# Cutting the last product of a kernel, and one early multiply, in two halves

## The chip, the cores and the metric

The kernel runs on one core of one Trainium2 chip. The metric is the device time of one execution in microseconds (us). The time of the kernel before is a median of 304.57 us over three runs (304.38 to 305.19).

## The reference

Eight batches of eight heads attend in chunks of 64 tokens. The result, 4608 rows of 512, goes through a bilinear feed-forward layer.

```python
scores = scale * np.matmul(q_c, k_c.transpose(0, 1, 2, 4, 3))     # chunks of 64
attn = softmax(scores)                                            # cut: max, exp, sum
out = np.matmul(attn, v_c)
x = out.transpose(0, 2, 1, 3).reshape(B * S, H * D)               # 4608 x 512
result = ((x @ w_a) * (x @ w_b)) @ w_out                          # d_ff = 1536
```

## The kernel before

The tokens are worked on in units of 256 and blocks of 512. TensorE (PE) does all products. From block 1 on, the output product of a block is a form of 2x2 block multiplication with seven products (`part(n, th)`, n from 0 to 6), whose sums are kept in the banks A, B and C of PSUM, the memory that TensorE writes its sums to. For the last block it is done for each half of 128 rows (`th`) by itself, which the code calls `one`.

The first place that the change touches is the end of the attention of a unit. Both VectorE multiplies write into `xT`, the feed-forward product's input; `m` runs over its four slices of 128 features, and the feed-forward product accumulates over these four slices (`kt`).

```python
def values(U):
    ...                                        # av[cl]: attention times v, in PSUM
    for cl in range(2):
        x = x_tiles[K][:, :, 256 * u:256 * u + 256]
        nc.vector.tensor_tensor(
            out=x.rearrange("p m (g c s) -> p m g c s", g=2, c=2)[:, :, :, cl, :],
            in0=av[cl],
            in1=rs[:, cl].rearrange("p m (g s) -> p m g s", g=2),
            op=MULT,
        )
```

The second place is the end of the kernel. The loop that comes last is `for n in (1, 2, 4, 3, 5, 6): for th in range(2): ends[th].part(n, th)`, so the last piece of work is n = 6 with th = 1:

```python
def part(self, n, th):
    ...                                        # t, a, w: bank, left and right operand
    c0 = 0 if one else th * 256
    for kt in range(HFT):                      # HFT = 6
        nc.tensor.matmul(
            t[:, c0:c0 + 256],
            a[:, kt, th * 128:th * 128 + 128],
            w[:, kt],
            start=n in (0, 4) and first and kt == 0,
            stop=last and kt == HFT - 1,
            skip_group_check=True,
        )
    if not last:
        return
    ...                                        # n = 0 to 4
    elif n == 5:
        ...                                    # the right columns of o0, on ScalarE
        for c in [th] if one else range(2):
            store(self.K, 0, c, self.o0[:, c])
    else:
        nc.vector.tensor_scalar(
            out=rows(self.o1, lo), in0=halves(self.C), scalar1=OUT_SCALE,
            scalar2=None, op0=MULT,
        )
        for c in [th] if one else range(2):
            store(
                self.K, 1, c, self.o1[:, c], lo if one else slice(0, DM),
                nc.scalar if one and th else nc.sync,
            )
    ...                                        # n = 3: right columns of o1, stored; C += u
```

The softmax here doesn't subtract the row's maximum and nothing guards it: scores larger than these inputs give would overflow.

## Time and profile before

| what | value | where it is read |
|---|---|---|
| span of the profiled execution | 301.92 us | head of the page |
| PE busy | 291.9 us, 97% | part 1 of the page |
| share of PE in the chain that ended last | 83% | part 4 |
| first feed-forward matmul | 17.68 us | timeline |
| PE idle for GpSimd's wb cast | 0.28 us at 32.84 | timeline |
| last product, first matmul to the end of the span | 3.91 us | timeline, span |

Three parts of the page of the kernel before: its head, its busy times, and its chain by engine.

```profile
span 301.9 us, 8590 instructions
...
PE 291.9 (97%) x3521; PEld 231.6 (77%) x3521; DVE 212.5 (70%) x341; ACT 196.6 (65%) x355; POOL 193.5 (64%) x180
...
PE 83%; DMA 6%; DVE 3%; SPq 3%; ACT 1%; POOL 1%; issue 1%; DVEq 0%; ACTq 0%
```

Next is the timeline of the kernel before, cut to the lines that matter for the front. The columns are the start, the duration (both us), the engine, the source line, the operation, output and inputs, the shapes, and the count of merged instructions. In square brackets are the idle time of the engine before it, and what ended that.

```profile
16.24 0.69 DVE L337 TENSOR_TENSOR xT<-pb,ln 128x512 f16<-128x512 f32 x1 [0.31 <-ACT ln L305]
...
16.94 0.69 DVE L337 TENSOR_TENSOR xT<-po,ln 128x512 f16<-128x512 f32 x1
...
17.68 1.02 PE L389 MATMUL pb<-xT,wb 128*128 128x512 f16 x4 [0.38 <-DVE xT L337]
...
28.67 1.04 POOL L213 CAST q_raw<-st 128x1024 bf16<-128x1024 f32 x1 [1.10 <-DMA st<-in_q_dram]
...
32.84 1.04 PE L389 MATMUL pb<-xT,wb 128*128 128x512 f16 x4 [0.28 <-POOL wb L120]
32.85 1.04 POOL L120 CAST wa<-st 128x1024 f16<-128x1024 f32 x1
...
33.63 0.53 DVE L135 TENSOR_TENSOR t<-wa 128x512 f16<-128x512 f16 x1
...
33.95 1.04 PE L389 MATMUL pc<-xT,wa 128*128 128x512 f16 x4
```

The last multiply (L337) starts at 16.94 and ends at 17.63; PE starts 0.05 us later. At 32.84 PE sits idle for 0.28 us until GpSimd has cast a weight tile, and at 33.95 it starts 0.06 us after the end of the wa cast of 32.85. Such places are read by which wait ends last, not by how busy an engine is.

The next view is the table of stretches: the stretch, its length, the busy time of each engine with its count of instructions, the granted PE clock, the mean busy share of the 16 DMA engines (over 1 where packets overlap), and GB/s.

```profile
14.00:24.00 10.00, 9.47 (x76) 4.24 (x74) 5.26 (x9) 4.68 (x9) 6.41 (x7) 1.00 1.07 369
24.00:30.00 6.00, 6.00 (x32) 2.72 (x31) 4.11 (x7) 2.27 (x4) 3.14 (x3) 1.00 1.20 251
30.00:36.00 6.00, 5.66 (x68) 2.76 (x65) 5.04 (x8) 3.08 (x6) 4.30 (x4) 1.00 1.12 337
298.50:300.70 2.20, 0.33 (x4) 0.05 (x1) 0.56 (x2) 0.00 (x0) 0.00 (x0) 1.00 0.96 358
```

From 14 to 36 us the mean share of the DMA engines stays over 1, and from 298.5 to 300.7 it is 0.96, so they hardly rest. The last view is the timeline of the tail. An eviction there is VectorE's scaled copy of finished sums from PSUM to SBUF, from which the store is read.

```profile
298.01 0.82 PE L575 MATMUL pa<-wot,ab_sb 128*128 128x256 f16 x6
298.21 0.43 DVE L608 TENSOR_SCALAR o_sb<-po 128x256 f32<-128x256 f32 x1 [0.67 <-PE po L575]
298.87 0.42 DVE L608 TENSOR_SCALAR o_sb<-pa 128x256 f32<-128x256 f32 x1 [0.23 <-PE pa L575]
299.32 0.37 ACTq L523 DMA_DIRECT2D out_dram<-o_sb  x1
```

Six matmuls of 256 columns, the eviction of 128x256, and the issue of the last store at 299.32; the span ends at 301.92. In between lie the time to the store's first packet, its packets and the end of the program.

### The profile page before, as it was taken

The page shows a single profiled execution, that of the slowest core. Times are in us where ns is not written, and L with a number is a line of the kernel's source. Part 1 is how long each engine was busy: PE and PEld are TensorE (multiplying, and loading weights), DVE is VectorE, ACT ScalarE, POOL GpSimd, SP SyncE. Part 2 cuts the span into 40 slices and gives each one's busy share as a digit, 9 for nine tenths or more (in the row PEclk, how much of TensorE's full clock was granted, in tenths as well). Part 3 has the DMA queues.
Part 4 walks back from the last instruction along what each step waited for, and adds up shares of the span by engine and source line. Part 5 has one row for each costly group of instructions (what it writes and reads, how often), then busy time and mean ns, then how long its engine had stood idle before and what let it go on. Part 6 is the DMA issues. An engine that isn't in the chain of part 4 may idle for free.

```text
span 301.9 us, 8590 instructions
## 1 busy us (share of the span) xinstructions
PE 291.9 (97%) x3521; PEld 231.6 (77%) x3521; DVE 212.5 (70%) x341; ACT 196.6 (65%) x355; POOL 193.5 (64%) x180
## 2 busy tenths in 40 slices
PE   6799999999999999999999999999999999999995
PEld 2344467766588888888888888888888888888884
DVE  3456766866887696769676967796679667965773
ACT  2743567348387759676877687768776877567532
POOL 0665758996999688908890888088817801790560
PEclk9999999999999999999999999999999999999999
DMA  7999999999999999895959395949631001100025
GB/s 233 303 376 275 289 336 342 246 205 214 224 235 269 209 237 275 189 228 174 215 114 240 138 210 124 229 144 207 123 87 72 2 2 69 72 1 3 2 78 200
DMA packets 140983, 54.29 MB, mean 180 GB/s; under 512 B 117136, under 2 KB 135056, under 8 KB 140944
## 3 DMA queue, kind: packets, MB, share of 16 engines
q1 hardware_dynamic: 140800, 53.62, 70.3%
q8 instruction: 27, 0.44, 0.6%
q10 hardware_dynamic: 144, 0.13, 0.1%
q14 instruction: 12, 0.10, 0.1%
HBM read 37.75 MB, written 9.44 MB: 156 GB/s over the span
## 4 chain that ended last, share of the span: by engine, by line
PE 83%; DMA 6%; DVE 3%; SPq 3%; ACT 1%; POOL 1%; issue 1%; DVEq 0%; ACTq 0%
PE pb L439 19%; PE pc L439 12%; PE pa L439 12%; PE po L575 12%; PE pq L575 10%; PE pb L643 3%; DMA st<-in_moe_w_b_dram 3%; DMA st<-in_moe_w_a_dram 2%; PE po L389 2%; PE pc L389 2%; PE pa L389 2%; PE pq L389 2%; DMA st<-in_v_dram 2%; PE pt L328 2%; PE pt L295 2%; SPq L194 1%
## 5 line engine op out<-in xcount | busy, mean ns | idle before, releaser
L519 POOL TENSOR_TENSOR so<-ab_sb 128x512 f16<-128x512 f16 x23 | 27.4, 1191 | 68.6 <-DVE ab_sb L489 68.6
L439 PEld LDWEIGHTS <-t 128*128 128x128 f16 x504 | 48.3, 98 | 8.8 <-issue 2.3
L439 PE MATMUL pb<-s,wa 128*128 128x256 f16 x336 | 50.5, 273 | 0.0
L439 PE MATMUL pa<-xT,wb 128*128 128x256 f16 x336 | 50.4, 273 | 0.0
L477 DVE TENSOR_TENSOR c_sb<-pc,v_sb 128x512 f32<-128x512 f32 x42 | 28.9, 687 | 25.4 <-ACT v_sb L450 25.4
L575 PEld LDWEIGHTS <-ab_sb 128*128 128x128 f16 x384 | 37.6, 98 | 4.7 <-issue 0.4
L439 PEld LDWEIGHTS <-wb 128*128 128x128 f16 x336 | 32.9, 98 | 4.0
L439 PEld LDWEIGHTS <-wa 128*128 128x128 f16 x336 | 31.8, 98 | 4.2 <-issue 0.2
L489 DVE SCALAR_TENSOR_TENSOR ab_sb<-pc,c_sb 128x512 f16<-128x512 f32 x42 | 28.9, 689 | 7.8 <-PE pc L439 6.3
L450 ACT COPY u_sb<-pb 128x512 f32<-128x512 f32 x42 | 24.7, 588 | 14.8 <-PE pb L439 14.7
L489 DVE SCALAR_TENSOR_TENSOR ab_sb<-pb,b_sb 128x512 f16<-128x512 f32 x42 | 29.0, 689 | 6.1 <-PE pb L439 5.2
L457 ACT COPY pb<-pa 128x512 f32<-128x512 f32 x42 | 24.0, 573 | 10.7 <-PE pa L439 10.3
L575 PEld LDWEIGHTS <-so 128*128 128x128 f16 x288 | 28.1, 98 | 3.4
L450 ACT COPY b_sb<-pa 128x512 f32<-128x512 f32 x42 | 25.0, 595 | 7.1 <-PE pa L439 7.1
L478 DVE TENSOR_TENSOR pc<-pc,u_sb 128x512 f32<-128x512 f32 x42 | 28.9, 688 | 0.0
L519 POOL TENSOR_TENSOR so<-so,ab_sb 128x512 f16<-128x512 f16 x23 | 27.1, 1180 | 1.7
L450 ACT COPY v_sb<-pb 128x512 f32<-128x512 f32 x42 | 24.6, 587 | 5.0 <-PE pb L439 4.4
L519 POOL TENSOR_TENSOR ab_sb<-ab_sb 128x512 f16<-128x512 f16 x23 | 26.9, 1172 | 0.0
L519 POOL TENSOR_TENSOR so<-ab_sb,so 128x512 f16<-128x512 f16 x23 | 26.2, 1170 | 0.0
L337 DVE TENSOR_TENSOR xT<-pt,ln 128x512 f16<-128x512 f32 x29 | 18.8, 686 | 10.1 <-PE pt L328 6.7
L439 PE MATMUL pc<-s,t 128*128 128x256 f16 x168 | 25.2, 273 | 0.2 <-DVE ab_sb L489 0.2
L439 PE MATMUL pc<-xT,t 128*128 128x256 f16 x168 | 25.2, 272 | 0.1
(129 smaller groups left out, 576.9 us busy)
## 6 DMA issues: line engine op xcount, KB each, us to landing
out_dram<-o_sb SPq DMA_DIRECT2D x34, 256.0 KB, 2.3
st<-in_v_dram SPq DMA_DIRECT2D x32, 256.0 KB, 4.6
st<-in_k_dram SPq DMA_DIRECT2D x25, 256.0 KB, 4.6
st<-in_q_dram SPq DMA_DIRECT2D x23, 256.0 KB, 3.9
st<-in_moe_w_b_dram SPq DMA_DIRECT2D x6, 512.0 KB, 7.1
st<-in_moe_w_a_dram SPq DMA_DIRECT2D x6, 512.0 KB, 6.9
st<-in_moe_w_out_dram SPq DMA_DIRECT2D x6, 512.0 KB, 6.4
st<-in_q_dram SPq DMA_DIRECT2D x4, 512.0 KB, 5.4
```

Source lines behind the costliest of these rows:

```text
L295: nc.tensor.matmul(sm[cl][j * 64:j * 64 + 64, :], ones[cl * 64:cl * 64 + 64, :], E[cl * 64:cl * 64 + 64, j].rearrange("p m g s -> p (m g s)"),
L337: nc.vector.tensor_tensor(out=x.rearrange("p m (g c s) -> p m g c s", g=2, c=2)[:, :, :, cl, :], in0=av[cl], in1=rs[:, cl].rearrange("p m ...
L389: nc.tensor.matmul(ps[n], w_ab[n, i][:, kt, o:o + 128], xT[:, kt, c0:c1], start=(kt == 0), stop=(kt == NKT - 1),)
L439: nc.tensor.matmul(t[:, h * 256:h * 256 + 256], w[:, kt, h * 128:h * 128 + 128], x[:, kt], start=start and h == 0 and kt == 0, stop=h == 1 ...
L450: nc.scalar.copy(out=t, in_=src)
L457: nc.scalar.copy(out=self.B, in_=self.A)
L477: nc.vector.tensor_tensor(out=self.c, in0=self.C, in1=self.v, op=ADD)
L478: nc.vector.tensor_tensor(out=self.C, in0=self.C, in1=self.u, op=ADD)
L489: nc.vector.scalar_tensor_tensor(out=self.dst[:, :, c0:c0 + 256], in0=t.rearrange("p (h n) -> p h n", h=2), scalar=AB_SCALE, in1=o.rearran ...
L519: (eng or nc.gpsimd).tensor_tensor(out=o, in0=x0, in1=x1, op=op)
L575: nc.tensor.matmul(t[:, c0:c0 + 256], a[:, kt, th * 128:th * 128 + 128], w[:, kt], start=n in (0, 4) and first and kt == 0, stop=last and ...
L643: nc.tensor.matmul(out_ps[K, tg], ab_tiles[K][:, ft, tg * 128:tg * 128 + 128], wo_sb[:, ft], start=(ft == 0), stop=(ft == NFT - 1),)
```

## The change

Its intent is to shorten two waits. The first feed-forward matmuls should start when half of `xT`'s slices are there. At the end, the eviction and the store of the first 128 columns should overlap the product of the second 128 columns, so that only half an eviction and half a store remain after the last matmul.

```diff
         for cl in range(2):
             x = x_tiles[K][:, :, 256 * u:256 * u + 256]
-            nc.vector.tensor_tensor(
-                ...
-            )
+            for m in (slice(0, 2), slice(2, 4)) if (U, cl) == (1, 1) else [slice(0, 4)]:
+                nc.vector.tensor_tensor(
+                    out=x.rearrange("p m (g c s) -> p m g c s", g=2, c=2)[:, m, :, cl, :],
+                    in0=av[cl][:, m],
+                    in1=rs[:, cl, m].rearrange("p m (g s) -> p m g s", g=2),
+                    op=MULT,
+                )
 ...
-            for kt in range(HFT):
-                nc.tensor.matmul(
-                    t[:, c0:c0 + 256],
-                    ...
-                )
-            if not last:
+            end = n == 6 and one and th == 1
+            for cols in (slice(0, 128), slice(128, 256)) if end else [slice(0, 256)]:
+                for kt in range(HFT):
+                    nc.tensor.matmul(
+                        t[:, c0:c0 + 256][:, cols],
+                        a[:, kt, th * 128:th * 128 + 128],
+                        w[:, kt, cols],
+                        ...                              # start, stop as before
+                    )
+                if end:
+                    nc.vector.tensor_scalar(
+                        out=rows(self.o1, cols), in0=self.C[:, cols], scalar1=OUT_SCALE,
+                        scalar2=None, op0=MULT,
+                    )
+                    store(
+                        self.K, 1, th, self.o1[:, th], cols, nc.scalar if cols.start else nc.sync
+                    )
+            if not last or end:
                 return
```

The store of the other row half (th = 0) stays on the Sync queue, as it was.

More of the change, by code (lines that the diff above doesn't have):

```diff
@@ L336, in values @@
             x = x_tiles[K][:, :, 256 * u:256 * u + 256]
-            nc.vector.tensor_tensor(
-                out=x.rearrange("p m (g c s) -> p m g c s", g=2, c=2)[:, :, :, cl, :],
-                in0=av[cl],
-                in1=rs[:, cl].rearrange("p m (g s) -> p m g s", g=2),
-                op=MULT,
-            )
+            for m in (slice(0, 2), slice(2, 4)) if (U, cl) == (1, 1) else [slice(0, 4)]:
[5 more added lines that the diff above has]
+                )
     def slot(s=None, f=None):
@@ L573, in part @@
             c0 = 0 if one else th * 256
-            for kt in range(HFT):
-                nc.tensor.matmul(
-                    t[:, c0:c0 + 256],
-                    a[:, kt, th * 128:th * 128 + 128],
-                    w[:, kt],
-                    start=n in (0, 4) and first and kt == 0,
-                    stop=last and kt == HFT - 1,
-                    skip_group_check=True,
-                )
-            if not last:
+            end = n == 6 and one and th == 1
[5 more added lines that the diff above has]
+                        w[:, kt, cols],
+                        start=n in (0, 4) and first and kt == 0,
+                        stop=last and kt == HFT - 1,
+                        skip_group_check=True,
+                    )
[8 more added lines that the diff above has]
+            if not last or end:
                 return
@@ L612, in part @@
                 for c in [th] if one else range(2):
-                    store(
-                        self.K, 1, c, self.o1[:, c], lo if one else slice(0, DM),
-                        nc.scalar if one and th else nc.sync,
-                    )
+                    store(self.K, 1, c, self.o1[:, c], lo if one else slice(0, DM))
             if n == (3 if one else 4):
```

## The prediction

> **What bounds the kernel.** The page of the profile gives PE 97% of a 301.9 us span, and the chain of waits is 83% PE. PE has almost no idle time between 46 and 289 us, and the change touches nothing there. It touches one wait near 17 us and the last 4 us.
>
> **Front: unit 1's last multiply in two halves.** The timeline shows VectorE's multiplies ending at 17.63 and the first feed-forward matmul starting at 17.68, after 0.38 us of PE idle put down to this multiply (128x512, 0.69 us). Split by m, the first half (128x256 operations take 0.42 us) ends near 17.36 and frees two of four accumulating matmuls (0.21 us each); the second half ends near 17.69. PE starts about 0.27 us earlier; VectorE pays about 0.07 us.
> I expect none of it to reach the end. PE next meets GpSimd's casts at 29.77 (a cast ending at 29.71), 32.84 (idle 0.28 us, wb cast) and 33.95 (wa cast). There the chain of waits runs: v load, v cast, w_b load, cast, issue, w_a load, cast. From 14 to 36 us the DMA engines are busy without a gap (share 1.04 to 1.27), so an earlier PE only waits longer. Value: 0, at most 0.15 us either way through the timing of VectorE against GpSimd.
>
> **Tail: the last product in column halves.** Before: six 256-column matmuls at 0.109 us each, from 298.01 to 298.84; VectorE evicts 128x256 until 299.29 (0.425 us); the Scalar queue issues a 128 KB store at 299.32, whose first packet runs at 300.23 and last ends at 300.72; the program ends at 301.9.
> After: twelve 128-column matmuls with twelve weight loads. The transposes show 128-column pairs at about 0.056 us, so each half costs about 0.34 us and PE work is unchanged. A 128x128 eviction is estimated at 0.29 us (687 ns for 512 columns, 425 for 256).
> What decides: both halves lie in one PSUM bank. The Trainium skill, "PSUM — Partial Sum Buffer", section "PSUM bank collisions raise a hardware error", says to guard PSUM by bank and quadrant, not by address. I expect (85%) the second half's matmuls to wait for the first half's eviction; no trace here shows it yet. Then: first half done 298.51, eviction 298.55 to 298.84, PE resumes 298.89, done 299.39, eviction to 299.72, issue 299.75: 0.43 us later than now. The last store is only 64 KB (estimate 0.22 us of packets: 27 ns per 512 bytes, 46 per 1024), so its last byte comes near 300.88: tail +0.16 us.
> Without that wait the second eviction ends near 299.16, 0.13 us earlier, but stores keep the DMA engines fully busy from 298.5 to 300.7, and 512-byte packets cost about 17% more per byte: gain 0 to 0.05 us.
>
> **Sum.** 304.57 + 0 (front) + 0.14 (tail, weighted) = 304.7 us; range 304.0 to 305.4, mostly the spread of runs. Faster by over 2%: 0.3%; within 2%: 99.4%; slower: 0.3%.
>
> **What shows it right.** First feed-forward matmul near 17.4; longer PE waits for GpSimd at 29.8 to 33, and matmuls from 34 us on within 0.1 us of now. In the tail a PE wait of about 0.38 us on VectorE between the halves, two evictions of 0.29 us, the Scalar queue's issue near 299.75.
> **What shows it wrong.** Matmuls after 46 us over 0.15 us earlier; or second-half matmuls following at once (no bank wait), last issue near 299.2.
> **What would make it wrong.** w_a/w_b loads issued earlier because a VectorE operation no longer delays the cast at 23.85 us (1.21 instead of 1.04 us); a chip spread above 0.2%.

## The result, and the profile after

The change runs at a median of 304.12 us (303.64 to 304.91, six runs), the kernel before at 304.48 us beside it (304.07 to 305.79, six runs). The ratio is 0.9985, with a 95% interval of 0.9961 to 1.0008. A ratio here is the mean time of one kernel's runs over that of the other's of the same rounds, so it is not quite the ratio of the medians. The interval holds 1. The profiled execution of the change has a span of 302.32 us, which is longer than the 301.92 of before, while the median is lower. That alone tells the reader not to explain the medians.

The page of the change, its head and busy times:

```profile
span 302.3 us, 8608 instructions
...
PE 292.4 (97%) x3527; PEld 231.9 (77%) x3527; DVE 210.0 (69%) x343; ACT 196.5 (65%) x355; POOL 193.3 (64%) x180
```

The timeline of the change, front, to be laid beside that of before:

```profile
17.17 0.76 DVE L338 TENSOR_TENSOR xT<-po,ln 128x256 f16<-128x256 f32 x2
...
17.65 1.02 PE L390 MATMUL pb<-xT,wb 128*128 128x512 f16 x4 [0.24 <-DVE xT L338]
...
28.43 1.04 POOL L213 CAST q_raw<-st 128x1024 bf16<-128x1024 f32 x1 [1.25 <-DMA st<-in_q_dram]
...
32.78 0.41 DVE L135 TENSOR_TENSOR t<-wa 128x512 f16<-128x512 f16 x1
...
32.89 1.20 POOL L120 CAST wa<-st 128x1024 f16<-128x1024 f32 x1
...
32.97 1.04 PE L390 MATMUL pb<-xT,wb 128*128 128x512 f16 x4 [0.36 <-POOL wb L120]
...
34.15 1.04 PE L390 MATMUL pc<-xT,wa 128*128 128x512 f16 x4 [0.15 <-POOL wa L120]
```

The two half multiplies are merged in one line; they start at 17.17 and PE starts 0.48 us later, where it was 0.74 us (16.94 to 17.68). So the step itself works. The clock time of the first matmul is nearly the same only because everything ahead of it ran 0.23 us later in this execution. Later on, PE waits 0.36 us for the wb cast (0.28 before) and a new 0.15 us for the wa cast, and it starts 0.06 us after the wa cast ends, as before. That cast takes 1.20 us instead of 1.04 here; VectorE's multiply `t<-wa` starts just before it (32.78), where in the kernel before it started well inside the cast (33.63). This comes back below.

The timeline of the change, tail:

```profile
298.02 0.50 PE L578 MATMUL pa<-wot,ab_sb 128*128 128x128 f16 x6
298.22 0.42 DVE L619 TENSOR_SCALAR o_sb<-po 128x256 f32<-128x256 f32 x1 [0.68 <-PE po L578]
298.56 0.28 DVE L587 TENSOR_SCALAR o_sb<-pa 128x128 f32<-128x128 f32 x1
298.90 0.49 PE L578 MATMUL pa<-wot,ab_sb 128*128 128x128 f16 x6 [0.38 <-DVE o_sb L587]
...
299.44 0.29 DVE L587 TENSOR_SCALAR o_sb<-pa 128x128 f32<-128x128 f32 x1 [0.59 <-PE pa L578]
299.76 0.37 ACTq L524 DMA_DIRECT2D out_dram<-o_sb  x1
```

Between the two groups of six matmuls PE waits 0.38 us for VectorE's eviction of the first half. The two halves do not overlap: product, eviction, product, eviction follow one another, and the last store is issued at 299.76 instead of 299.32.

### The profile page after: what moved, and what is told of

It is laid out like the page before. It is cut to its first block, busy times and chain, and to the rows that moved or that the text cites. A ratio compares the mean times of both kernels' runs of the same rounds, so it can differ in the third digit from the quotient of the medians.

```text
span 302.3 us, 8608 instructions
## 1 busy us (share of the span) xinstructions
PE 292.4 (97%) x3527; PEld 231.9 (77%) x3527; DVE 210.0 (69%) x343; ACT 196.5 (65%) x355; POOL 193.3 (64%) x180
## 4 chain that ended last, share of the span: by engine, by line
PE 83%; DMA 5%; SPq 4%; DVE 3%; POOL 1%; ACT 1%; issue 1%; DVEq 0%; ACTq 0%; POOLq 0%
PE pb L440 19%; PE pc L440 12%; PE pa L440 12%; PE po L578 12%; PE pq L578 10%; PE pb L651 3%; DMA st<-in_k_dram 3%; DMA st<-in_moe_w_b_dram 2%; PE po L390 2%; PE pc L390 2%; PE pa L390 2%; PE pq L390 2%; PE pt L328 2%; PE pt L295 2%; SPq L112 1%; SPq L194 1%
## 5 line engine op out<-in xcount | busy, mean ns | idle before, releaser
L440 PE MATMUL pb<-s,t 128*128 128x256 f16 x168 | 25.3, 273 | 0.0
```

The source lines that it names most:

```text
L440: nc.tensor.matmul(t[:, h * 256:h * 256 + 256], w[:, kt, h * 128:h * 128 + 128], x[:, kt], start=start and h == 0 and kt == 0, stop=h == 1 ...
```

## The experiments

Twelve runs were made, in three lots, each beside the kernel before on the same chip, with five rounds (but for the last one, a single look). All tail marks are counted from the first matmul of the last product; the tables take the start of the last issue on the Scalar queue, the first packet of that queue, the end of the last data packet of any queue, the last landing (the last completion of a semaphore, which tells the program that a store's data have arrived), and the end of the span. The marks are differences of rounded times, so a last digit can be off by one.

| run | last issue | its first packet | last data | last landing | end (tail) | landing to end |
|---|---|---|---|---|---|---|
| before | 1.31 | 2.22 | 2.71 | 3.06 | 3.91 | 0.84 |
| before again | 1.32 | 2.22 | 2.71 | 3.06 | 3.91 | 0.85 |
| the change | 1.74 | 2.61 | 2.95 | 3.35 | 4.30 | 0.95 |
| the change again | 1.73 | 2.60 | 2.94 | 3.34 | 4.29 | 0.95 |
| tail alone | 1.74 | 2.61 | 2.95 | 3.35 | 4.30 | 0.95 |
| change, seven more stores | 1.73 | 2.61 | 2.95 | 3.37 | 4.22 | 0.85 |
| tail in two banks | 1.20 | 2.38 | 2.71 | 3.18 | 4.02 | 0.84 |
| eviction and store in halves alone | 1.38 | 2.37 | 2.71 | 3.17 | 4.02 | 0.85 |
| early stores alone | 1.32 | 2.20 | 2.69 | 3.05 | 3.90 | 0.85 |
| candidate | 1.20 | 2.11 | 2.65 | 3.11 | 4.02 | 0.91 |

The tail repeats within 0.02 us from one execution to the next, and that is what makes it usable. For the front, the second table gives in each run the time from the start of the last multiply to the first feed-forward matmul; when that matmul ran; the wa cast of about 33 us; and the first matmul of unit 2's feed-forward, after which PE has hardly a gap.

| run | multiply to first matmul | first matmul at | wa cast start and duration | matmuls behind the wa cast at | unit 2 at |
|---|---|---|---|---|---|
| before | 0.74 | 17.68 | 32.85, 1.04 | 33.95 | 42.21 |
| before again | 0.74 | 17.82 | 32.96, 1.04 | 34.06 | 42.32 |
| tail alone | 0.75 | 17.79 | 33.54, 1.04 | 34.63 | 42.90 |
| tail in two banks | 0.74 | 17.70 | 32.55, 1.04 | 33.65 | 41.91 |
| eviction in halves | 0.75 | 17.66 | 32.85, 1.04 | 33.95 | 42.21 |
| early stores | 0.74 | 18.22 | 33.12, 1.04 | 34.21 | 42.86 |
| the change | 0.48 | 17.65 | 32.89, 1.20 | 34.15 | 42.42 |
| the change again | 0.48 | 17.45 | 32.52, 1.04 | 33.61 | 41.88 |
| seven more stores | 0.48 | 18.16 | 33.82, 1.32 | 35.19 | 43.46 |
| front alone, again | 0.47 | 17.52 | 33.81, 1.27 | 35.13 | 43.40 |
| candidate | 0.47 | 17.72 | 33.21, 1.11 | 34.38 | 42.64 |
| front later | 0.74 | 18.16 | 33.37, 1.03 | 34.46 | 42.72 |

In every run the matmuls behind the wa cast start 0.05 to 0.06 us after that cast ends. The cast itself took 1.03 or 1.04 us in all seven traces without the split and 1.11 to 1.32 us in four of the five with it. In exactly these four, VectorE's `t<-wa` started before the cast or at the same time; in the other eight it started after the cast did. So where the cast is stretched, it overlaps at its start with that VectorE operation, and PE's matmuls behind it come up to 0.28 us later. Whether the split brings this order about was not tested.

### The two parts apart

**Front alone.** The kernel before with the first half of the diff and nothing else.

> Unit 1's last multiply in two halves, the tail as before. Theory (the earlier start is absorbed where PE next meets GpSimd's casts): the first feed-forward matmul follows the start of the last multiply by about 0.48 us instead of 0.74, but the waits of PE for GpSimd between 29 and 34 us grow, the matmul group after the last wa cast there starts where the loads put it, and the ratio to the kernel before is 1.000 within 0.001. Rival (the 0.27 us pass through to the end): ratio 0.9991, and all matmuls from 34 us on 0.27 us earlier against the span's start. Either way the tail, from the first matmul of the last product to the end of the span, takes 3.91 us as before.

Five runs of 303.32 to 304.81 us; ratio 1.0012 (0.9985 to 1.0038). The profiled run, however, took 599.67 us, and its profile is of no use for the front. The groups of that run, and its clock:

```profile
L440 PE MATMUL pa<-xT,wb 128*128 128x256 f16 x336 | 96.8, 444 | 0.0
L440 PE MATMUL pb<-s,wa 128*128 128x256 f16 x336 | 94.7, 450 | 0.0
```

The means (after the busy time) are 444 and 450 ns, where the kernel before has 273 ns in the same groups; 592.7 us of the 597.9 us span are PE busy. From one of these matmuls to the next there are 222 ns where the kernel before has 109 (medians of the starts in the two traces; the means above hold more than this spacing). PE thus ran at about half its rate from the beginning to the end, although the recorded granted clock was 1.000. It is left out of every comparison and comes back at the end.

**Tail alone.** The kernel before with the second half of the diff and nothing else.

> The last product in column halves, stored apart; the front as before. Theory (the bank wait makes the tail longer): PE waits about 0.38 us for VectorE between the halves, the Scalar queue issues about 1.74 us after the last product's first matmul instead of 1.31, and the tail from that matmul to the end of the span takes 4.2 to 4.3 us instead of 3.91; ratio about 1.001. Rival (the halves make the tail shorter, and the 0.36 us by which the change's median is lower comes from here): tail at most 3.9 us, ratio 0.9988.

Median 304.03 us against 303.80; ratio 1.0011 (0.9984 to 1.0038). The tail is 4.30 us, as the theory said: 0.40 us longer than before, with the 0.38 us wait between the halves. The rival, that the halves shorten the tail, is out.

**The change again.** Not an edit: the change as it is, on the same chip as its parts.

> The whole change once more, on the same chip as its parts. Theory: tail 4.2 to 4.3 us as with the tail alone, front as with the front alone, ratio to before 1.000 to 1.002. Rival (the change is really faster by the 0.15% that its first six runs showed): ratio 0.9985 again.

Median 304.21 us against 303.80; ratio 1.0010 (0.9987 to 1.0033). Tail 4.29, front 0.48. The 0.9985 did not come back. Neither ratio is clear of 1, so what is shown is only that the lower median of the first six runs is no property that repeats.

### What the wait between the halves costs

**Two banks, first version.** The second half's product goes to another bank; its eviction adds the part that had been summed up before, which one small VectorE operation keeps in SBUF. Meant as below, but the store had slipped under the `elif`, so that the second half was never stored.

> As the tail alone, but the second half's product goes to another PSUM bank, whose eviction adds the part accumulated before (kept in SBUF by one more 128x128 VectorE operation before the last products). Twelve weight loads, 64 KB stores and 512-byte packets stay; only the wait goes. Theory (bank wait costs): no PE wait between the halves, second half done about 0.83 us after the last product's first matmul, issue about 1.2 us after it, tail 3.85 to 4.0 us, so 0.25 to 0.4 us less than the tail alone and about what it was before, as the stores' packets already fill the DMA engines. Rival (twelve small matmuls with their weight loads, or 512-byte packets, cost the time): the tail stays at 4.2 to 4.3 us without the wait.

The result was wrong (relative error not a number), by that slip. Its times (ratio 1.0006) are not used, as a store is missing.

**Two banks, mended.** On top of the tail alone:

```diff
+                apart = end and cols.start == 128
+                if apart:
+                    t = bank(psum_c)[:, :256]
 ...
-                        start=n in (0, 4) and first and kt == 0,
+                        start=(n in (0, 4) and first or apart) and kt == 0,
 ...
+                if apart:
+                    nc.vector.scalar_tensor_tensor(
+                        out=rows(self.o1, cols), in0=t[:, cols], scalar=OUT_SCALE,
+                        in1=self.kept[:, cols], op0=MULT, op1=ADD,
+                    )
-                if end:
+                elif end:
                     nc.vector.tensor_scalar(...)
+                if end:
                     store(...)
 ...
+                if one and th == 1:                      # n = 3, after C += u
+                    self.kept = self.temp("c_sb")
+                    nc.vector.tensor_scalar(
+                        out=self.kept[:, 128:256], in0=self.C[:, 128:256], scalar1=OUT_SCALE,
+                        scalar2=None, op0=MULT,
+                    )
```

> The two-bank tail once more, with the second half's store, which the first version had left out by a slip (its unwritten rows made the result not a number). No PE wait between the halves, the last issue about 1.20 us after the last product's first matmul (1.74 with one bank, 1.31 before). Theory (the bank wait is what costs): the tail from that matmul to the span's end is 3.75 to 3.95 us, at least 0.35 less than the 4.29 to 4.34 of the tail alone. Rival (weight loads, 512-byte packets or the extra store cost it): 4.1 us or more.

Correct; median 303.83 us against 303.82, ratio 0.9995 (0.9976 to 1.0014). The timeline of this run, tail:

```profile
297.89 0.50 PE L580 MATMUL pa<-wot,ab_sb 128*128 128x128 f16 x6
...
298.23 0.50 PE L580 MATMUL pc<-wot,ab_sb 128*128 128x128 f16 x6
298.44 0.28 DVE L594 TENSOR_SCALAR o_sb<-pa 128x128 f32<-128x128 f32 x1
298.76 0.29 DVE L589 SCALAR_TENSOR_TENSOR o_sb<-pc,c_sb 128x128 f32<-128x128 f32 x1
299.09 0.37 ACTq L523 DMA_DIRECT2D out_dram<-o_sb  x1
```

The second group of six follows the first after 0.34 us with no idle time, and both products and both evictions overlap as the change had meant. With the same twelve weight loads, the same 64 KB stores and the same 512-byte packets, the tail is 4.02 us, 0.28 us shorter than the tail alone. Not all of that is the wait. The last landing comes 0.17 us sooner (3.18 instead of 3.35); the rest, 0.11 us between the landing and the end, comes from the order in which semaphores are looked at, which has changed with the stores (see below, where the change with that order mended has a tail of 4.22 us). So the wait is worth 0.17 to 0.20 us, and the small matmuls and packets are cleared of that much. The size that was expected, at least 0.35 us and a tail of at most 3.95 us, is missed. The issue came 0.11 us earlier than before (1.20 against 1.31), but its first packet came at 2.38 instead of 2.22, the last data at the same 2.71, and the last landing 0.12 us later than before. Which store lands last is in the view of the DMA issues of this run (size, and time from issue to landing):

```profile
out_dram<-o_sb SPq DMA_DIRECT2D x1, 64.0 KB, 1.9
out_dram<-o_sb ACTq DMA_DIRECT2D x1, 64.0 KB, 2.0
```

The Sync queue's half is issued at 1.11 and lands at 3.01; the Scalar queue's is issued at 1.20 and lands last, at 3.18.

**Eviction and store in halves alone.** The kernel before, with the product whole:

```diff
+                parts = (slice(0, 128), slice(128, 256)) if one and th else [lo]
+                for cols in parts:
                     nc.vector.tensor_scalar(
-                        out=rows(self.o1, lo), in0=halves(self.C), ...
+                        out=rows(self.o1, cols), in0=halves(self.C)[..., cols], ...
                     )
+                    if one and th:
+                        store(..., cols, nc.scalar if cols.start else nc.sync)
```

> The last product whole as before, but its eviction and its store in column halves. No matmul waits for an eviction, as both come after the product. Theory: last issue about 1.38 us after the last product's first matmul, 0.07 later than before; the extra store again makes the last landing the one whose semaphore is looked at early (about 0.1 us more between landing and end); the store of half the size lands some 0.15 us sooner after its issue: tail 3.9 to 4.05 us. Rival (two stores instead of one are the cost, not the bank wait): tail 4.2 us or more.

Median 304.23 us against 303.82; ratio 1.0007 (0.9984 to 1.0029). The tail is 4.02 us, in the range, and with no bank wait there is nothing of the 4.2 us of the rival. But it came out differently from what the theory said: landing to end is 0.85 and not 0.95, and instead the last landing is at 3.17 where it was 3.06. In this run and in the one before, the store that lands last is the one on the Scalar queue, as in the change (the Sync queue's half lands at 3.01), but here it has kept the semaphore that is looked at last, and the Sync queue's half has the additional one. So the eviction and the store cut into two cost 0.11 us at the end by themselves. Last data to last landing takes 0.46 to 0.47 us there and 0.35 us before; why it does was not separated further.

### The rest of the tail

**Seven more stores.** The Sync queue looks at the completion semaphores of the stores, one after another, before the program may end. In the view of its waits, the columns are who waited, for whom, the total us, the times, and the longest. Before:

```profile
SPq L959 <- DMA out_dram<-o_sb: 1.8, 4, 0.6
```

and in the change:

```profile
SPq L967 <- DMA out_dram<-o_sb: 1.6, 1, 1.6
```

Before, four waits, the last of them for the last store. In the change one wait of 1.6 us, after which the trace still shows two looks at other stores of about 0.06 us each. The eight semaphores are handed out in turn, and the one store more had moved the last store to the next one. To test it, seven more stores were added far from the end:

```diff
 def store(K, u, c, o_sb, cols=slice(0, DM), eng=nc.sync):
     r0 = K * BLK + 256 * u + 128 * c
-    eng.dma_start(out=out[r0:r0 + 128, cols], in_=o_sb[:, cols])
+    whole = [cols]
+    if K in (3, 4) and 4 * (K - 3) + 2 * u + c < 7:
+        whole = [slice(0, 256), slice(256, 512)]
+    for cut in whole:
+        eng.dma_start(out=out[r0:r0 + 128, cut], in_=o_sb[:, cut])
```

> The whole change, with seven stores of blocks 3 and 4, far from the end, cut into two each. The eight completion semaphores are handed out in turn; with eight stores more than before in all, the last store has the same semaphore as before again, the last one that the Sync queue looks at. Theory (the change's one extra store moved the last landing to a semaphore looked at early, with two more looks of about 0.06 us behind it): last landing to the span's end 0.84 to 0.86 us as before (0.95 in the change), tail 4.15 to 4.22 us instead of 4.29 to 4.31; the PE wait of 0.38 us stays. Rival (the 0.11 us belongs to the small last store or the Scalar queue's late issue): 0.95 us and 4.30 us still.

Median 304.40 us against 303.93; ratio 1.0010 (0.9988 to 1.0031). Landing to end is back at 0.85 us, and the tail is 4.22 us, both as expected, with the same issue and the same last data as in the change. The waits of this run:

```profile
SPq L971 <- DMA out_dram<-o_sb: 1.6, 5, 0.6
```

Five waits with the last one ending last again. So the 0.10 us between the last landing and the end is the order in which semaphores are looked at, not the small store itself. The candidate below fits it: there one more look is behind the last landing, and landing to end is 0.91 us. In two banks the last store has the semaphore looked at last as well, so about 0.1 of the 0.28 us between the tail alone and two banks is this order. The 0.39 us by which the change lengthens the tail thus come apart: 0.11 for eviction and store in halves (3.91 to 4.02), 0.20 for the wait in one bank (4.02 to 4.22), and 0.08 for the order of the semaphores (4.22 to 4.30).

**Early stores alone.** Is it the stores in front that keep the last one from landing sooner? The left columns of o0 are done at n = 1, and the kernel before stores them only with the right ones at n = 5. Storing them at once takes 256 KB from the end (and six cut stores keep the last semaphore):

```diff
             elif n == 1:
                 ...                                      # left columns of o0
+                if one:
+                    store(self.K, 0, th, self.o0[:, th], lo)
 ...
-                    store(self.K, 0, c, self.o0[:, c])
+                    store(self.K, 0, c, self.o0[:, c], hi if one else slice(0, DM))
```

> The kernel before with the early stores alone (and six earlier stores cut, for the last semaphore): product, eviction and last store whole, issue at 1.31 us. Theory: last data at 2.55 to 2.65 us, tail 3.75 to 3.85 us; so the two banks in the candidate are worth 0.1 us only with the backlog gone. Rival (no backlog effect): 2.71 and 3.91 us as before.

Median 304.02 us against 303.93; ratio 0.9987 (0.9962 to 1.0013). The Sync queue's packets are now done at 2.16 us instead of 2.32, yet the last data ends at 2.69 and the tail is 3.90: the rival is right and the expectation missed. The last store's first packet comes 0.88 us after its issue (0.91 before), with and without the other stores, and its 128 KB then take 0.49 us. Issuing the last store earlier (two banks) left the last data at 2.71, and taking the backlog away leaves it at 2.69, so either alone gains at most 0.02 us there.

**Candidate.** Front split, two banks and early stores together (and five cut stores).

> A candidate to beat both: the front split, the last product in halves in two banks, and the first column halves of the last block's rows stored 4 us earlier, when they are done, in place of together with the second halves; five earlier stores cut in two to keep the last semaphore. Theory (the stores' backlog on the DMA engines, then the bank wait, then the semaphore order set the tail): last issue 1.20 us after the last product's first matmul, first packet 0.9 us after that issue instead of 1.18 with the full backlog, last data at 2.45 to 2.5 us (2.71 before), tail 3.6 to 3.75 us; ratio 0.999. Rival (the last store's fixed latency alone sets the end, the backlog does not count): last data at 2.7 us, tail 3.9 us.

Correct; median 304.64 us against 303.93, ratio 1.0013 (0.9986 to 1.0039): not a version that beats anything. The issue at 1.20 and its first packet 0.91 us later came as expected. But last data is at 2.65, not below 2.50, and the tail is 4.02. The 64 KB of the Scalar queue were done at 2.45; it is the first half's store, on the Sync queue, that is last. The Sync queue had issued stores at 0.21 and 0.71 us, and could issue this one only at 1.22, after the second half's, although its eviction had ended at 0.83. Sync needs about 0.5 us from one store to the next here. (The ratio says little of the tail: in the profiled execution PE also lost about 1 us between unit 2 and the tail, 0.4 us of it in a wait for GpSimd that the profile of before does not have; why was not looked into.) The two halves on exchanged queues would be the next thing to try; it was not run.

### The front

**Front later.** The kernel before, with the first matmul pushed the other way:

```diff
+            if (U, cl) == (1, 1):
+                idle = c_pool.tile([128, 512], FP32, name="b_sb")
+                nc.vector.tensor_copy(out=idle, in_=av[0].rearrange("p m g s -> p (m g s)"))
             nc.vector.tensor_tensor(...)                 # unit 1's last multiply
```

> The kernel before, with one more VectorE copy of 128x512 ahead of unit 1's last multiply, so that the first feed-forward matmul starts about 0.6 us later against the multiplies before it: twice the change's step, the other way. Theory (PE has about 0.5 us of idle time for GpSimd's casts near 33 us, and the loads decide when it goes on): the matmuls after the last wa cast there still start 1.1 to 1.25 us after that cast's start, PE's idle time for the casts falls to nearly nothing, the ratio is 1.000 within 0.0015. Rival (a shift of the first matmul goes through to the end): these matmuls 1.6 us or more after the cast's start, ratio 1.002.

Median 303.94 us against 303.82; ratio 0.9998 (0.9978 to 1.0019). The timeline of this run:

```profile
16.82 0.68 DVE L339 COPY b_sb<-pb 128x512 f32<-128x512 f32 x1
...
17.42 0.68 DVE L340 TENSOR_TENSOR xT<-po,ln 128x512 f16<-128x512 f32 x1
...
18.16 1.02 PE L392 MATMUL pb<-xT,wb 128*128 128x512 f16 x4 [0.87 <-DVE xT L340]
...
33.37 1.03 POOL L120 CAST wa<-st 128x1024 f16<-128x1024 f32 x1
...
33.47 1.04 PE L392 MATMUL pb<-xT,wb 128*128 128x512 f16 x4 [0.36 <-POOL wb L120]
...
34.46 1.04 PE L392 MATMUL pc<-xT,wa 128*128 128x512 f16 x4
```

The copy pushes the multiply by 0.60 us, and PE starts at 18.16. The matmuls behind the wa cast still start 1.09 us after that cast's start, as the theory said and not 1.6 us after. But PE's idle time for the casts did not fall to nothing: it is 0.36 us at 33.47, because GpSimd's loads were late in this execution too (wa cast at 33.37). So the run shows that PE is gated by the cast; the cast at 33.37 lies within the 32.55 to 33.54 of the other runs without the split, so one trace can't tell whether the later front had delayed it. It doesn't measure how much slack there was, and 0.5 us in the mean of six runs would lie at the edge of what their interval can see.

**Front alone, again.**

> The front alone again, since the first profile of it fell into an execution in which PE ran at half its rate throughout (599.67 us, 1 of 6 runs; the others 303.3 to 304.8). Theory: first matmul 0.48 us after the last multiply's start (0.74 before), the matmuls after the last wa cast 1.10 us after that cast's start as in every other kernel, tail 3.91, ratio 1.000 within 0.0015, no run at half rate. Rival (the half rate comes with this kernel): such runs again. Rival (the step goes through): ratio 0.9991.

Median 303.54 us against 303.82; ratio 0.9991 (0.9969 to 1.0014). The ratio agrees with the rival to the digit, and with 1 as well; the first lot gave 1.0012 for the same code. The one trace, of the slowest of the six runs (304.66 us), can't decide what the mean does, but it shows the stages:

```profile
17.05 0.76 DVE L338 TENSOR_TENSOR xT<-po,ln 128x256 f16<-128x256 f32 x2 [0.23 <-ACT ln L314]
...
17.52 1.02 PE L390 MATMUL pb<-xT,wb 128*128 128x512 f16 x4 [0.33 <-DVE xT L338]
...
33.81 1.27 POOL L120 CAST wa<-st 128x1024 f16<-128x1024 f32 x1 [0.21 <-DMA st<-in_moe_w_a_dram]
...
35.13 1.04 PE L390 MATMUL pc<-xT,wa 128*128 128x512 f16 x4 [0.44 <-POOL wa L120]
```

PE starts 0.47 us behind the multiply, at 17.52, earlier than in any run without the split. At 35.13 it is later than in any of those, with 0.44 us of PE idle put down to the wa cast, which began only at 33.81 after GpSimd had waited for its load. The matmuls come 1.32 us after the cast's start, not the 1.10 expected, as this is one of the stretched casts (1.27 us). The tail is 3.91 us.

**Before again.** Not an edit, one look.

> The kernel before, once more with a profile, to see what its own stages do from one execution to the next. Theory (the loads of the first 40 us carry the spread, the tail does not): tail 3.9 us within 0.03, the matmuls after the last wa cast 1.10 us behind that cast's start, the cast's start anywhere from 32.5 to 33.8 us.

303.55 us. Tail 3.91, and the matmuls 1.10 us behind the wa cast's start, as expected; the cast at 32.96.

## Why the prediction was right or wrong

**The time.** 304.12 us lies in the range of 304.0 to 305.4, and "within 2%" holds. The point, 304.7, said slightly slower; the ratios of the complete change are 0.9985 and 1.0010, and neither is clear of 1. The hit is no test: the range is as wide as the spread of runs, and the kernel before (304.48) lies in it too. The change's lower median in those six runs was chance as far as is known. The traces show that the tail is slower by 0.39 us, which would be a ratio of 1.0013 (0.39 over 304). The front cannot be summed over runs so exactly.

**Front, the step itself: right.** 0.27 us was predicted; 0.74 became 0.47 to 0.48 us, in five traces with the split against seven without.

**Front, absorbed: right as far as the traces go, but one sign missed.** In all twelve traces of the second table, the matmuls behind the wa cast follow that cast and not the first matmul. But the sign "matmuls from 34 us on within 0.1 us of now" failed in the change's own profile: they start at 34.15 instead of 33.95, because the wa cast took 1.20 us instead of 1.04 and started 0.04 us later. The prediction had allowed up to 0.15 us for the timing of VectorE against GpSimd; the stretched casts cost 0.07 to 0.28 us. Unit 2's start ranges from 41.88 to 43.46 us with the split and from 41.91 to 42.90 without it, and the second earliest first matmul of all, 17.52, went with the second latest start of unit 2, 43.40. That the casts decide this, and the loads before them, is shown by the waits at the casts. What makes the loads vary from one execution to the next was not tested. A mean gain or loss of the order of 0.2 us from the split is not excluded by the twelve traces nor by any interval.

**Tail, the bank wait: right.** The wait of 0.38 us, the evictions at 298.56 and 299.44 and the issue at 299.76 came within 0.01 us of what was predicted (298.55, 299.43, 299.75). The Trainium skill's rule, "PSUM — Partial Sum Buffer", section "PSUM bank collisions raise a hardware error", to guard PSUM by bank and quadrant and not by address, was what led to it. The trace agrees in so far as columns 128 to 255 waited for a read of columns 0 to 127 of the same bank, and did not when they were in another bank. No run shows a collision; the wait is one that the program contains.

**Tail, its size: the term that was wrong.** The prediction said "tail +0.16 us". It is +0.39 us. By the first table, taken apart: last issue +0.43 (predicted 0.43); issue to last data 1.21 instead of 1.40, so -0.19, where -0.27 was reckoned, because the 64 KB took 0.34 us and not the estimated 0.22 (and their first packet came 0.87 us after the issue, not 0.91); last data to landing +0.05 (0.40 instead of 0.35), not reckoned; and landing to end +0.10, not reckoned, which the seven more stores show to be the order of the semaphores. (The 0.22 us are eight packets of 27 ns one after another. For the 128 KB before, eight of 46 ns would be 0.37 us where the trace has 0.49, so about 0.12 us was left out in both.) The estimate took the packets' durations as all that a store takes and the program's end as fixed.

**Tail without the wait: right for the last data, wrong for the tail.** "Gain 0 to 0.05" was said for a build without a bank wait, as the stores keep the DMA engines busy. In two banks the last data ended at 2.71 us as before. But with the backlog reduced it still ended at 2.69: the 0.88 us from issue to first packet bind just as much. And eviction and store in halves made it a loss of 0.11 us at the end, which the prediction hadn't.

## What to carry to other kernels

Cutting a product into column halves, so that one half's eviction overlaps the other's matmuls, needs two PSUM banks; in one bank the halves run one after another, and the extra round costs more than the smaller last eviction saves. Here two banks only took the wait away; with a tail of 4.02 us they were still no better than the whole product's 3.91. At the end of a kernel, look for all the limits that end together (fixed delay of the last store, backlog, issue rate of a queue, order of the final semaphore looks) before shortening one of them. And where a stage's gain is smaller than the run's spread, compare marks within traces, several of each kernel, rather than medians.

## What the Trainium skill lacked or had wrong

- "DMA: Bandwidth & Descriptors", section "Issuing engines are not separate DMA queues", says that issuing from several engines only saves the sequencer's issue time, "which is usually small relative to the DMA itself". At the end of this kernel it is not small: the Sync queue's stores are about 0.5 us apart (0.21, 0.71 and 1.22 us in the candidate), while the packets of a 64 KB store take about 0.34 us, and it was this spacing that set the candidate's last data.
- None of its pages says that the order in which a program looks at its completion semaphores costs time at the end: from landing to end it is 0.85 us where the last store's semaphore is looked at last, 0.91 with one more look behind it and 0.95 with two.
- "PSUM — Partial Sum Buffer" tells that it is to be guarded by bank and quadrant, not by address, but not what that costs a product split by columns. Here it is a PE wait of 0.38 us, of which 0.17 to 0.20 us reach the end of the tail.
- "TensorE: Matmul & The Clock Gate", section "Part 1: The HAM clock gate (the "warmup" mystery)", describes a half rate at the beginning that sustained activity ends, and warns that recorded throttle events have been unreliable. One run here kept about half the rate for all of its 597.9 us, with PE 99% busy and a recorded granted clock of 1.000; the warning fits that record, but nothing was found that explains the rate, and six more runs of the same code didn't show it.
